# A gated recurrence and an FFT convolution on one core: x2 and its spectrum in halves, the filter with doubled columns, a re-tuned planner

## The chip, the cores and the metric

The kernel runs on one core of a Trainium2 chip. A core has a matrix engine (PE, whose weight loads are listed apart as PEld), a vector engine (DVE), an activation engine (ACT), a general engine (POOL, GpSimd) and a queue that issues transfers (SP). Each engine works off its own instructions in order and waits on semaphores for the others. The metric is the time of one execution on the device, in microseconds.

## The reference

Two layers follow each other. The first is a gated recurrence over time; the second multiplies two projections of its output with a circular convolution of a third, the convolution being written as a product of Fourier transforms over the whole sequence.

```
B, S, D = 4, 6272, 256
sig = 1 / (1 + exp(-f_logit));  f = lb + (1 - lb) * sig;  i = 1 - f
h = 0
for t in range(S):
    h = f[:, t] * h + i[:, t] * x[:, t];  hs[:, t] = h
x1, x2, x3 = split(hs @ w_proj)                      # D -> 3 D
x2 = irfft(rfft(x2, axis=1) * rfft(filter, axis=0))  # length S
out = (x1 * x2 * x3) @ w_out
```

## The kernel before

**The transform.** S = 6272 is split as 128 x 49. A transform over the sequence is a transform of length 128 over m and one of length 49 over r, both written as matrix products with small tables (D1, FT, VA, VB, ID). The 256 channels are kept as pairs: NEP = 128 pairs, cut into 16 units of UE = 8 pairs.

**The stages of a batch.** There are four batches; each goes through these stages:

- `hgrn`: in 13 chunks of 512 steps, f_logit and x are loaded (buffers FL and XT, NX = 4 deep), ACT takes the sigmoid, POOL multiplies it into x, PE turns both to channels by time (L292), ACT makes the forget gate (L304), and a DVE scan (L309) writes h into the two outer parts of HA. POOL then copies each piece into the middle of HA as well (L260, the wraps), so that strided reads can run past the end.
- `phase_p`: 98 matmuls (L587) make x2 for all 49 r and both halves of the channels of h. The weights are h, read with a stride of 49 elements; the moving operand is W2 with 256 columns. DVE or ACT copies the results into X2.
- `phase_f1`: 128 matmuls (L602) transform over m. Their copies fill A, which is the middle of HA: all 16 units lie side by side where the wraps were. `mini` (L617 to L627) then handles the zero frequency of all pairs at once.
- `units`: for each unit, the spectrum of the filter comes from DRAM into Hu, PE transforms over r (L646, F2), DVE multiplies with Hu into PP (L656), POOL fills the zero frequency (L649), PE transforms back over r (L666), and a copy puts the result into Th. Th is a view of X2's memory. Beside the units `gate` works: PE projects h to x1 and x3 (L338), ACT evicts both (L348), and POOL multiplies them into zt (L352). The list GATES says which chunks of the gate go with which unit.
- `phase_o`: in 13 groups of 4 r, PE transforms back over m (L692), DVE multiplies with zt into ys (L699), PE projects with Wo (L709), a copy scales into one of two output buffers, and a store goes out. The first buffer is osb0; the second is the tail of X2, so it appears as X in the profile (`out_dram<-X`).

**Before the first batch** `prepare` builds the tables and the filter's spectrum: it loads the filter, rotates it (L517), transforms it over m with 128 matmuls of 128 columns in fp32r (L531), over r with 64 matmuls (L547), and writes it to DRAM. It shares memory with later stages: raw pieces and results lie in the middle of HA, the transformed filter in a pool that is closed before the buffers of the later stages are opened.

**The order** is not written by hand. Every operation is registered with a guessed cost per engine, the names it reads and writes, and the PSUM banks it takes. `Plan.emit` is a list scheduler: it walks a simulated time, always takes the operation that can start first (ties by the length of the chain that hangs on it, called the level), chooses between ACT and DVE where a copy can run on either, and emits each engine's instructions in that order. `emit` is called twice: once for `prepare` and the first `hgrn`, once for all that follows. The engines then run this fixed order with the real durations. A mis-guessed cost gives an order in which an engine waits with other work queued behind.

Two lines matter for the waits: the copy into X2 also writes the name of the second output buffer, and reads Th.

```
e, both(xv[:, :, r0:r0 + rn]), PS[...]), r=["Th"], w=[("x2", g), ("x2o", g)], src=pp)
r=[("osb", k)] + ([("x2o", i) for i in range(14)] if k else []), kb=128 * rn)
```

Of the kernel before, what the change touches and what calls it, by code (L numbers as in the profile page):

```python
# [9 lines left out]
F32 = mybir.dt.float32  # L10
# [3 lines left out]
AOP = mybir.AluOpType  # L14
# [13 lines left out]
NX = 4  # L28
NCHK = 13

AFTER = (0,)

GATES = [[0, 1, 2], [3, 4], [5, 6], [7, 8], [9, 10], [11, 12]] + [[]] * 10
XR = 10
NEP = 128
# [6 lines left out]
EW = NEP * 128  # L42
# [13 lines left out]
class Plan:  # L56
# [11 lines left out]
    SLACK = 0.0  # L68

    def __init__(self):  # L70
        self.ops, self.writer, self.readers = [], {}, {}
        self.free = {e: 0.0 for e in self.LAT}
        self.bank = [0.0] * 8
        self.dma = 0.0
        self.table = None

    def op(self, cost, fn, r=(), w=(), kb=0.0, table=None, take=0, src=None):
# [9 lines left out]
        if src is not None:  # L87
            preds.add(src)
            self.ops[src]["users"].append(me)
        self.ops.append(dict(cost=cost, fn=fn, preds=preds, kb=kb, table=table, end=None,  # L90
                             eng=None, succ=[], take=take, src=src, users=[], at=None))
# [9 lines left out]
    def ready(self, o, e):  # L101
        at = 0.0
        for p in o["preds"]:
            q = self.ops[p]
            lat = 0.0 if q["kb"] else (self.OWN if q["eng"] == e else self.LAT)[q["eng"]]
            at = max(at, q["end"] + lat)
        return at

    def room(self, n):

        best = None
        for b in range(0, 8, n):
            if None not in self.bank[b:b + n]:
                key = (max(self.bank[b:b + n]), n == 1 and self.bank[b ^ 1] is not None, b)
                if best is None or key < best:
                    best = key
        return best

    def held(self, i):

        return any(self.ops[p]["end"] is None and p != i
                   for j in self.ops[i]["users"] for p in self.ops[j]["preds"])

    def emit(self):
        ops = self.ops
        todo = [i for i, o in enumerate(ops) if o["end"] is None]
        for i in reversed(todo):
            o = ops[i]
            c = min(o["cost"].values()) + (2.6 + o["kb"] / 300.0 if o["kb"] else 0.2)
            o["level"] = c + max((ops[j]["level"] for j in o["succ"]), default=0.0)  # L130
        left = {i: sum(ops[p]["end"] is None for p in ops[i]["preds"]) for i in todo}
        cand = {i for i in todo if not left[i]}
        while cand:
            best = None
            rooms = {n: self.room(n) for n in (1, 2)}
            for e, f in self.free.items():
                can = []
                for i in cand:
                    o = ops[i]
                    if e not in o["cost"]:  # L140
                        continue
                    at = max(f, self.ready(o, e))
                    if o["take"]:
                        if rooms[o["take"]] is None or self.held(i):
                            continue
                        at = max(at, rooms[o["take"]][0])
                    if o["table"] and self.table and o["table"] != self.table:
                        at += 1.3
                    can.append((at, -o["level"], i))
                if can:  # L150
                    first = min(can)[0] + self.SLACK
                    pick = min((c for c in can if c[0] <= first), key=lambda c: c[1:])
                    o = ops[pick[2]]
                    key = (pick[0] + (o["cost"][e] if len(o["cost"]) > 1 else 0.0) * 0.01,
                           pick[1], pick[2], e, pick[0])
                    if best is None or key < best:
                        best = key
            assert best is not None
            i, e, at = best[2:]
            o = ops[i]  # L160
            o["eng"] = e
            o["end"] = self.free[e] = at + o["cost"][e]
            if o["table"]:
                self.table = o["table"]
            if o["kb"]:
                self.dma = max(self.dma, o["end"] + 0.6) + o["kb"] / 300.0
                o["end"] = self.dma + 1.0
            if o["take"]:
                o["at"] = b = rooms[o["take"]][2]
                self.bank[b:b + o["take"]] = [None] * o["take"]  # L170
                o["fn"](e, b)
            elif o["src"] is not None:
                q = ops[o["src"]]
                o["fn"](e, q["at"])
                q["uses"] = q.get("uses", 0) + 1
                q["done"] = max(q.get("done", 0.0), o["end"] + self.LAT[e])
                if q["uses"] == len(q["users"]):
                    self.bank[q["at"]:q["at"] + q["take"]] = [q["done"]] * q["take"]
            else:
                o["fn"](e)  # L180
            cand.remove(i)
            for j in o["succ"]:
                left[j] -= 1
                if not left[j]:
                    cand.add(j)
# [3 lines left out]
def kernel(  # L189
# [35 lines left out]
    A = HA[:, S:S + EW].rearrange("m (e r k) -> m e r k", r=2, k=64)  # L225
# [4 lines left out]
    x1s = konst.tile([128, 2, CH], F32, name="x1s")  # L230
    x3s = konst.tile([128, 2, CH], F32, name="x3s")
# [37 lines left out]
    def hgrn(b):  # L269
        for c in range(NCHK):  # L270
# [6 lines left out]
            for dst, src, t in ((ft, f_logit, ("ft", k)), (xt, x, ("xt", k))):  # L277
                op({"SP": 0.5}, lambda e, dst=dst, src=src, t0=t0, n=n: nc.sync.dma_start(
                    dst, src[b, t0:t0 + n, :].rearrange("(j p) d -> p j d", p=128)),
                   w=[t], kb=n)  # L280
            op({"ACT": 0.1 + 0.213 * nb}, lambda e, ft=ft: nc.scalar.activation(  # L281
                ft, ft, AF.Sigmoid, scale=-1.0), r=["sin"], w=[("ft", k)], table="sigmoid")
            op({"POOL": 0.1 + 0.535 * nb}, lambda e, xt=xt, ft=ft: nc.gpsimd.tensor_tensor(  # L283
                xt, xt, ft, op=AOP.mult), r=[("ft", k)], w=[("xt", k)])

            late = [("U", AFTER[min(c, len(AFTER) - 1)])] if b else []
            for kh in range(2):
                cols = slice(kh * 128, kh * 128 + 128)

                def turn(e, p, src, cols=cols, nb=nb):  # L290
                    for j in range(nb):
                        nc.tensor.transpose(PS[:, p, j * 128:(j + 1) * 128], src[:, j, cols],  # L292
                                            iden[:])
                sT = op({"PE": 0.108 * nb}, lambda e, p, f=turn, s=ft: f(e, p, s),
                        r=[("ft", k), "iden"] + late, w=["qT"], take=1)
                uT = op({"PE": 0.108 * nb}, lambda e, p, f=turn, s=xt: f(e, p, s),
# [6 lines left out]
                op({"ACT": 0.24 + n / 1200.0}, lambda e, p, fT=fT, n=n, kh=kh:  # L303
# [4 lines left out]
                op({"DVE": 0.07 + 2.25 * n / 1000.0}, lambda e, p, h=h, fT=fT, n=n, init=init:  # L308
# [9 lines left out]
                op({"POOL": 0.1 + (z - a) / 1000.0},  # L318
# [5 lines left out]
    def gate(b, u):  # L324
        z = zt
        for c in GATES[u]:
# [4 lines left out]
            for jb in range(2):  # L331
                x13 = []
                for i in range(2):
                    js = slice(i * 256 + jb * 128, i * 256 + jb * 128 + 128)

                    def mm(e, p, js=js, t0=t0, n=n):
                        for kh in range(2):
# [3 lines left out]
                    x13.append(op({"PE": 2 * n / 2400.0}, mm,  # L341
                                  r=hn + ["W13", ("F", u) if u else "qT"], w=["qX"], take=1))
                j = count["s"] % 2
                count["s"] += 1
                xs = [t[:, j, 0:n] for t in (x1s, x3s)]
                for i in range(2):
                    op({"ACT": 0.15 + n / 1200.0}, lambda e, p, xs=xs[i], n=n, i=i:
                       nc.scalar.activation(  # L348
                           xs, PS[:, p, 0:n], AF.Copy, scale=1.0 if i else ZS),
                       w=[("x1s", j, i)], src=x13[i])  # L350
# [438 lines left out]
```

## Time and profile before

| what | value |
|---|---|
| time, median of 3 runs | 593.94 us (581.37 to 595.5) |
| span of the profiled run | 590.6 us |
| PE busy | 505.9 us (86%) |
| DVE busy | 458.7 us (78%) |
| ACT busy | 413.2 us (70%) |
| POOL busy | 391.7 us (66%) |
| moved by DMA | 117.57 MB, mean 199 GB/s |

PE is the busiest engine by this table, but its matmuls are pipelined, so busy time counts the same stretch for several of them and a stretch at a lower clock counts in full. The other engines' busy time can be taken as it stands. The heaviest groups are:

```profile
L352 POOL TENSOR_TENSOR zt<-x1s,x3s 128x490 f16<-128x490 f32 (+1 forms) x104 | 203.8, 1980 | 48.1 <-ACT x3s L348 47.5
L656 DVE TENSOR_TENSOR PP<-PS,Hu 98x1008 f16<-98x1008 f32 x128 | 146.0, 1198 | 8.5 <-ACT x3s L348 3.7
L309 DVE TENSOR_TENSOR_SCAN HA<-fTs,HA,PS 128x512 f16<-128x512 f32 (+1 forms) x96 | 112.3, 1201 | 18.1 <-ACT fTs L304 10.1
L338 PE MATMUL PS<-HA,W 128*128 128x490 f16 (+1 forms) x416 | 101.4, 369 | 5.1 <-ACT X L250 2.7
L531 PE MATMUL PS<-D1r,f 128*128 128x128 f32 x128 | 28.1, 390 | 1.3 <-ACT f L250 1.2
```

A row reads: line, engine, operation, what it writes and reads with shapes, how often, then busy microseconds and the mean nanoseconds of one, then the idle time just before these instructions and what ended most of it. A matmul's mean includes the time it spends in the pipeline, so what one costs in a dense stretch has to be read from the starts of neighbours in the timeline.

### The profile page before, as it was taken

How to read it: one execution, taken by the hardware profiler on the slowest of the kernel's cores; microseconds unless marked ns; L12 is line 12 of the kernel's file. 1: busy time of each engine (PE TensorE's matmuls, PEld its weight loads, DVE VectorE, ACT ScalarE, POOL GpSimd, SP SyncE). 2: the span in 40 equal slices, each digit the busy share in tenths (PEclk: the TensorE clock that was granted, in tenths of full speed). 3: DMA queues.
4: the chain of work that ended last, by engine and by line, in shares of the span. 5: the costliest groups of instructions: out<-in, count | busy, mean ns of one | idle time of the engine just before them, and what ended most of it. 6: DMA issues, size and time to landing. Idle time of an engine off the chain costs nothing.

```text
span 590.6 us, 12576 instructions
## 1 busy us (share of the span) xinstructions
PE 505.9 (86%) x4821; PEld 375.7 (64%) x4821; DVE 458.7 (78%) x442; ACT 413.2 (70%) x577; POOL 391.7 (66%) x362
## 2 busy tenths in 40 slices
PE   1656999988799888698999898888999989989893
PEld 1555777676456788475557775674568878645582
DVE  8776644868798978379999894388988988999761
ACT  4578543569588567687886778786886778878553
POOL 3618640358999847955996778907995783599600
PEclk9978555999999989989999999798999999999897
DMA  8998434492457989900558999103559971045155
GB/s 297 373 360 284 135 111 134 135 307 83 126 156 203 319 264 347 336 1 28 165 168 250 326 369 374 72 1 109 162 172 326 367 279 51 3 136 166 29 214 223
DMA packets 73038, 117.57 MB, mean 199 GB/s; under 512 B 4366, under 2 KB 55634, under 8 KB 72978
## 3 DMA queue, kind: packets, MB, share of 16 engines
q1 hardware_dynamic: 72978, 116.77, 60.0%
q8 instruction: 38, 0.62, 0.5%
q14 instruction: 22, 0.18, 0.1%
HBM read 84.54 MB, written 32.11 MB: 198 GB/s over the span
## 4 chain that ended last, share of the span: by engine, by line
PE 36%; DMA 12%; ACT 8%; DVE 7%; POOL 6%; issue 3%; SPq 0%; ACTq 0%; DVEq 0%
PE PS L338 8%; DMA out_dram<-X 7%; PE PS L666 6%; PE PS L292 6%; POOL zt L352 5%; PE PS L646 5%; PE PS L587 4%; PE PS L709 4%; DMA FL<-in_f_logit_dram 3%; DVE HA L309 2%; ACT X L250 2%; DVE HA L255 2%; PE PS L692 2%; ACT X L252 2%; PE PS L602 1%
## 5 line engine op out<-in xcount | busy, mean ns | idle before, releaser
L352 POOL TENSOR_TENSOR zt<-x1s,x3s 128x490 f16<-128x490 f32 (+1 forms) x104 | 203.8, 1980 | 48.1 <-ACT x3s L348 47.5
L283 POOL TENSOR_TENSOR XT<-XT,FL 128x1024 f32<-128x1024 f32 (+1 forms) x52 | 117.1, 2257 | 55.3 <-ACT FL L281 32.1
L656 DVE TENSOR_TENSOR PP<-PS,Hu 98x1008 f16<-98x1008 f32 x128 | 146.0, 1198 | 8.5 <-ACT x3s L348 3.7
L309 DVE TENSOR_TENSOR_SCAN HA<-fTs,HA,PS 128x512 f16<-128x512 f32 (+1 forms) x96 | 112.3, 1201 | 18.1 <-ACT fTs L304 10.1
L338 PE MATMUL PS<-HA,W 128*128 128x490 f16 (+1 forms) x416 | 101.4, 369 | 5.1 <-ACT X L250 2.7
L250 ACT CAST X<-PS 128x784 f16<-128x784 f32 (+2 forms) x89 | 88.1, 1002 | 12.4 <-PE PS L587 5.5
L304 ACT ACTIVATE fTs<-PS,nomc 128x512 f32<-128x512 f32 (+1 forms) x104 | 68.0, 663 | 40.0 <-PE PS L292 20.6
L348 ACT ACTIVATE x1s<-PS 128x490 f32<-128x490 f32 (+1 forms) x104 | 60.4, 581 | 41.8 <-POOL zt L352 28.3
L260 POOL COPY HA<-HA 128x512 f16<-128x512 f16 (+3 forms) x100 | 58.3, 600 | 32.0 <-DVE HA L309 31.3
L292 PE MATMUL PS<-iden,XT 128*128 128x128 f32 x392 | 65.6, 290 | 11.8 <-POOL XT L283 5.0
L338 PEld LDWEIGHTS <-W 128*128 128x128 f16 x416 | 35.3, 98 | 62.0 <-issue 37.1
L292 PE MATMUL PS<-iden,FL 128*128 128x128 f32 x392 | 65.2, 290 | 7.7 <-ACT FL L281 4.0
L699 DVE TENSOR_TENSOR ys<-PS,zt 128x1024 fp32r<-128x1024 f32 (+1 forms) x52 | 58.8, 1151 | 15.6 <-PE PS L692 11.7
L709 PE MATMUL PS<-Wo,ys 128*128 128x256 f32 x392 | 61.0, 301 | 8.7 <-ACT X L252 4.7
L666 PEld LDWEIGHTS <-PP 98*128 98x128 f16 x1024 | 51.2, 98 | 21.2 <-POOL PP L649 7.2
L255 DVE CAST X<-PS 128x1024 f16<-128x1024 f32 (+2 forms) x27 | 38.7, 1450 | 33.5 <-DMA out_dram<-X 24.1
L281 ACT ACTIVATE FL<-FL 128x1024 f32<-128x1024 f32 (+1 forms) x52 | 52.5, 1011 | 16.5 <-DMA FL<-in_f_logit_dram 16.3
L348 ACT ACTIVATE x3s<-PS 128x490 f32<-128x490 f32 (+1 forms) x104 | 59.9, 576 | 2.9 <-PE PS L338 2.8
L709 PEld LDWEIGHTS PS<-Wo,ys 128*128 128x128 f32 x392 | 51.6, 196 | 15.0 <-ACT X L252 6.0
L292 PEld LDWEIGHTS PS<-iden,XT 128*128 128x128 f32 x392 | 46.6, 147 | 19.6 <-POOL XT L283 6.2
L666 PE MATMUL PS<-VA,PP 98*128 98x98 f16 x512 | 52.8, 208 | 6.3 <-POOL PP L649 3.4
L587 PE MATMUL PS<-W,HA 128*128 128x256 f16 x392 | 50.1, 289 | 9.0 <-ACT X L250 3.9
(91 smaller groups left out, 678.5 us busy)
## 6 DMA issues: line engine op xcount, KB each, us to landing
Hu<-H SPq DMA_DIRECT2D x64, 392.0 KB
FL<-in_f_logit_dram SPq DMA_DIRECT2D x48, 512.0 KB
XT<-in_x_dram SPq DMA_DIRECT2D x48, 512.0 KB
out_dram<-osb SPq DMA_DIRECT2D x24, 512.0 KB
out_dram<-X SPq DMA_DIRECT2D x24, 512.0 KB
HA<-in_moe_filter_fft_dram SPq DMA_DIRECT2D x12, 512.0 KB
H<-HA SPq DMA_DIRECT2D x16, 196.0 KB
H<-HA SPq DMA_DIRECT2D x32, 98.0 KB
```

Of the source, the lines that this page charges most:

```text
L250: nc.scalar.copy(dst, src)
L283: op({"POOL": 0.1 + 0.535 * nb}, lambda e, xt=xt, ft=ft: nc.gpsimd.tensor_tensor(xt, xt, ft, op=AOP.mult), r=[("ft", k)], w=[("xt", k)])
L292: nc.tensor.transpose(PS[:, p, j * 128:(j + 1) * 128], src[:, j, cols], iden[:])
L304: nc.scalar.activation(fT, PS[:, p, 0:n], AF.Identity, scale=nomc[:, kh:kh + 1], bias=1.0),
L309: nc.vector.tensor_tensor_scan(h, fT, PS[:, p, 0:n], init, op0=AOP.mult, op1=AOP.add),
L338: nc.tensor.matmul(PS[:, p, 0:n], W13[:, kh, js], HA[:, HB[kh] + t0:HB[kh] + t0 + n], start=(kh == 0), stop=(kh == 1))
L348: nc.scalar.activation(xs, PS[:, p, 0:n], AF.Copy, scale=1.0 if i else ZS),
L352: zz=z[:, jb, :, m0:m0 + nm]: nc.gpsimd.tensor_tensor(zz, xs[0].rearrange("p (m r) -> p r m", r=Q), xs[1].rearrange("p (m r) -> p r m", r= ...
L587: nc.tensor.matmul(pp[:, r - r0, :], HA[:, n0:n0 + Q * 127 + 1:Q], W2[:, kh, :], start=(kh == 0), stop=(kh == 1))
L656: nc.vector.tensor_tensor(PP[:TB, k, o, :, :, 1:64], px.unsqueeze(1).broadcast_to([TB, 2, UE, 63]), hh[:, :, :, 1:64], op=AOP.mult)
L666: nc.tensor.matmul(PS[:, ib + o, pr * TB:(pr + 1) * TB], PP[:TB, k, o, n, 2 * pr:2 * pr + 2, :], v[:TB], start=(n == 0), stop=(n == 1))
L709: nc.tensor.matmul(po[:, i, :], y[:, kh, i * 128:(i + 1) * 128], Wo[:, kh, :], start=(kh == 0), stop=(kh == 1))
```

## The change

It has six parts.

1. **Own memory.** X2, PP, Hu and zm move out of the late pool into the constant one. Th, the second output buffer and X2 no longer share memory. To pay for it X2 holds only half of the pairs, NX goes from 4 to 3, and A holds four units (NA = 4) in a part of HA's middle that no wrap copy writes.
2. **x2 and its spectrum in halves.** `phase_p(b, v)` makes one half of the channels at a time, with 128 columns of W2, in 7 groups of 7 r. `phase_f1`, `mini` and `unit` follow for the two quarters of that half; each quarter is four units.
3. **The filter's transform over m has doubled columns.** The table D1r is held twice side by side, a matmul has 256 columns, and the copy reads one half of them. Four such matmuls fill two PSUM banks where eight did. The results leave through two buffers in Hu where there were four in HA, and raw pieces have five places where there were six.
4. **One emit.** Filter, first recurrence and all that follows are planned together. The late pool (zt, Th, ys, x1s, x3s, the output buffers) opens inside an operation that waits for the filter's matmuls.
5. **The gate** is free to run wherever the planner puts it: GATES and the waits on units go.
6. **Priorities.** Each operation has a kind, and a table LEAD adds a number per kind and batch to its level. Some guessed costs are new: the gate's product on POOL 0.12 + 3.7 n/1000 in place of 0.12 + 2.2 n/1000 (n = 490), the projection 0.32 per pair in place of 0.34.

The diff, cut to its core:

```diff
-NX = 4
+NX = 3
-GATES = [[0, 1, 2], [3, 4], [5, 6], [7, 8], [9, 10], [11, 12]] + [[]] * 10
+NA = 4
+NP = 2
+NH = 4
+AT = 6144
...
+    LEAD = {
+        "load": (2, 0, -5, -60), "sig": (-10, 21, -13, 0), "u": (9, 12, 0, 85),
...
+            level[i] = way[i] + self.LEAD.get(o["kind"], (0,) * 4)[o["batch"]]
...
-    A = HA[:, S:S + EW].rearrange("m (e r k) -> m e r k", r=2, k=64)
+    A = HA[:, S + AT:S + AT + NA * UE * 128].rearrange("m (e r k) -> m e r k", r=2, k=64)
+    X2 = konst.tile([128, NEP // 2 * PW + 16], F16, name="X2")
+    PP = konst.tile([128, NP, 2, 2, UE, 64], F16, name="PP")
+    Hu = konst.tile([128, NH, 2, 2, UE * 64], F16, name="Hu")
...
-                op({"POOL": 0.12 + 2.2 * n / 1000}, lambda e, xs=xs,
+                op("z", {"POOL": 0.12 + 3.7 * n / 1000}, lambda e, xs=xs, jb=jb, m0=m0, nm=nm:
...
-        hws = [HA[:, S + a:S + a + 1024].rearrange("p (a n) -> p a n", a=2)
-               for a in (6144, 7168, 8192, 9216)]
+        hws = [Hu[:, h, 0] for h in (NH - 2, NH - 1)]
...
-        D1r = tmp.tile([128, 128], F32R, name="D1r")
+        D1r = tmp.tile([128, 2, 128], F32R, name="D1r")
...
-                for i in range(UE):
-                    nc.tensor.matmul(pa[:, i, :], f2[:, (u * UE + i) * PW:(u * UE + i) * PW + 128], D1r[:],
-                                     start=True, stop=True)
+            for h in range(2):
+                def first(e, pb, j=u * UE + h * 4):
+                    pa = PS[:, pb:pb + 2].rearrange("m a (i c) -> m (a i) c", c=256)
+                    for i in range(4):
+                        nc.tensor.matmul(pa[:, i, :], f2[:, (j + i) * PW:(j + i) * PW + 128],
+                                         D1r[:].rearrange("m x k -> m (x k)"), start=True, stop=True)
...
-    def phase_p(b):
-        for g, r0 in enumerate(range(0, Q, 4)):
-                        nc.tensor.matmul(pp[:, r - r0, :], HA[:, n0:n0 + Q * 127 + 1:Q],
-                                         W2[:, kh, :], start=(kh == 0), stop=(kh == 1))
+    def phase_p(b, v):
+        for g in range(7):
+                        nc.tensor.matmul(pp[:, r - 7 * g, :], HA[:, n0:n0 + Q * 127 + 1:Q],
+                                         W2[:, kh, v * 128:v * 128 + 128],
+                                         start=(kh == 0), stop=(kh == 1))
+            pp = op("P", {"PE": 0.118 * 7}, mm, r=hn + E(0, AT) + E(AT + 4096, EW), take=2)
...
+    def spectrum(b):
+        for v in range(2):
+            phase_p(b, v)
+            for q in range(2 * v, 2 * v + 2):
+                for u in range(q * NA, q * NA + NA):
+                    phase_f1(b, u)
+                mini(b, q)
+                for u in range(q * NA, q * NA + NA):
+                    unit(b, u)
...
-        osb = [cv.tile([128, 4, 256], F32, name="osb0"),
-               X2[:, NEP * TB:NEP * TB + 2048].bitcast(F32).rearrange("p (r e) -> p r e", e=256)]
+            late["osb"] = [cv.tile([128, 4, 256], F32, name=f"osb{i}") for i in range(2)]
```

## The prediction

> **What bounds the kernel now.** I read the slices of the whole span first, then the engines' busy time per stage, then the chain of waits and the timeline where the stages look thin, and last single rows for durations.
>
> ```profile
> PE   1656999988799888698999898888999989989893
> DVE  8776644868798978379999894388988988999761
> PEclk9978555999999989989999999798999999999897
> ...
> PE 36%; DMA 12%; ACT 8%; DVE 7%; POOL 6%; issue 3%; SPq 0%; ACTq 0%; DVEq 0%
> ```
>
> One slice is 14.8 us. Slices 5 to 7 (59 to 103 us) have PE at 9 but its clock at 5: that is the filter. DVE drops to 3 and 4 around 240 and 362 us. No engine has more than 36% of the chain: the kernel is not held by one unit but by stages with different limits. By stage (columns: stretch, its length, busy us of PE, PEld, DVE, ACT, POOL, clock, DMA share, GB/s):
>
> ```profile
> 59.00:112.00 53.00, 52.54 (x244) 39.37 (x244) 28.38 (x25) 23.87 (x29) 19.78 (x33) 0.58 0.41 125
> 117.00:252.00 135.00, 115.33 (x1183) 86.43 (x1184) 106.54 (x94) 98.82 (x142) 110.38 (x90) 0.99 0.74 236
> 252.00:379.00 127.00, 115.14 (x1151) 83.36 (x1151) 100.54 (x89) 96.91 (x140) 99.89 (x85) 0.96 0.61 204
> 379.00:490.00 111.00, 102.52 (x1100) 76.59 (x1098) 99.41 (x87) 85.75 (x122) 77.31 (x73) 0.98 0.58 195
> 490.00:590.00 100.00, 85.48 (x941) 61.08 (x939) 74.51 (x65) 65.96 (x93) 52.67 (x45) 0.93 0.33 114
> ```
>
> The head (until the first x2 matmul, L587, at 116 us), then four batches of 135, 127, 111 and 100 us from x2 to x2. The middle ones lose time where x2 is made:
>
> ```profile
> 250.84 2.78 DVE L255 CAST X<-PS 128x1024 f16<-128x1024 f32 x2 [9.59 <-DMA out_dram<-X]
> ...
> 372.58 6.71 PE L587 MATMUL PS<-W,HA 128*128 128x256 f16 x32 [2.71 <-ACT x1s L348]
> 377.96 2.86 DVE L255 CAST X<-PS 128x1024 f16<-128x1024 f32 x2 [14.55 <-DMA out_dram<-X]
> ```
>
> The copies of the new x2 wait until a store of the old output has read its source, because the second output buffer lies in X2; DVE sits idle 9.6 and 14.6 us for it. Ahead of the second one PE also waits for the gate's evictions (x1s), which wait for GpSimd's products at 1.98 us each (L352).
>
> [...] 0.50 from 75 to 105 us although PE is never idle there. [...] the trace has 56 (24 L602 matmuls, from 133.69 to the next start at 135.03) and 113 (95 of L587 in 10.73). [...] the weight loads of L587, read at a stride of 49 elements, take 142 ns, those of L602, contiguous, 98.
>
> ```profile
> L587 PEld LDWEIGHTS <-HA x392: 141/142/168, 116.4 to 501.0; 128*128 128x128 f16 x196
> L602 PEld LDWEIGHTS <-X x512: 95/98/100, 133.7 to 512.8; 128*128 128x128 f16 x171
> ```
>
> **The filter.** Its m-DFT (L531) runs 128 fp32r matmuls of 128 columns:
>
> ```profile
> 69.88 3.68 PE L531 MATMUL PS<-D1r,f 128*128 128x128 f32 x16
> 107.79 1.11 PE L531 MATMUL PS<-D1r,f 128*128 128x128 f32 x8
> ```
>
> At half clock 16 start within 3.47 us (the next row begins at 73.35), 217 ns each; at full clock 8 within 0.95 (next at 108.74), 119 ns. Projection matmuls (L709, same type, 256 columns) take 131 ns (8 from 361.30 to 362.35) in stages whose clock stays at 1.00. So twice the columns cost 12 ns each, and the array streams 256 columns in the slot where it now streams 128. I take it that this keeps the clock up; no row of before shows it directly, so this is the first unknown. Full-clock stage: 128 x 0.131 = 16.8; 64 second-stage matmuls (L547, 4 in 0.63) 10.1; transposes. The instruction order of the changed kernel has 108 transposes between first filter DFT and last against 52, with 92 ahead of it against 128; 108 x 0.11 = 11.9. Sum 38.8 us of PE. DVE and ACT there: 32 copies of 512 columns at 0.65 (the 512-column row of L250 and L255), 16 of 1024 at 1.12, and for 108/8 pieces a scan 1.27, a forget gate 0.69 and half a sigmoid 1.06: 20.8 + 17.9 + 17.1 + 9.3 + 7.2 = 72, or 36 each. With 3 us of slack, 42 us. It starts earlier: 12 input loads stand ahead of the last filter load in the queue against 16, 2.1 MB less at 360 GB/s, so 53.5 us instead of 59.4. First x2 at 95 us instead of 116. At half clock the same PE work is 70 us or more: x2 at about 120. Only two buffers (in Hu) remain for the filter's results against four; a pair must go out within 2 x 2.6 us. A store held back in the SP queue by a load that waits for one of only 3 input buffers would hold the second-stage matmuls behind it. I allow that in the range.
>
> **A batch, by engine.** DVE: scans 122.1/4 = 30.5, products 36.5, y 14.7, zero frequency 2.5 before and about 5 after (12 short instructions in place of 3, at 0.3 to 0.6). ACT: forget gate 17.0, x1 and x3 30.1, sigmoid 13.1. Shared copies: x2 18.7, A 17.1, Th 13.1, output 12.8; x2 becomes 14 of 896 columns in place of 13, the same. Sum 206 before, 208 after, so 104 each. POOL: (203.8 + 117.1 + 58.3 + 23.4)/4 = 101; the wipe of X2's gaps per batch (0.4) goes. PE at its start-to-start times: transposes 196 x 0.11 = 21.6, x1 and x3 104 x 0.207 = 21.5, x2 98 x 0.113 = 11.1, F1 128 x 0.056 = 7.2, F2 64 x 0.126 = 8.1, inverse 256 x 0.044 = 11.3 and 196 x 0.035 = 6.9, projection 98 x 0.131 = 12.8: 100.5. Here the change adds: x2 becomes 196 matmuls of 128 columns with 196 strided weight loads. The matmul alone would give 0.056; but its load takes 142 ns, and the transposes, whose loads take 140, run at 0.11. So 11 to 21.8 us; I take 0.085, 16.7, and PE 106 a batch. That is the bound of a batch.
>
> **What the edits release.** Own output and Th buffers remove the 9.6 and 14.6 us waits above. X2 in halves and four slots of A that no wrap copy overlaps let units start when a quarter of the spectrum is there, and let scans and their copies of the next batch run beside units. The order shows this: when the first output inverse (L692) is issued, 88 to 112 of the next batch's 196 transposes are done, against 24 to 52 before. What now stands at 50 to 66 us of transposes, scans and loads (DMA share 0.9) shrinks to some 35 us. GpSimd's product is planned at 1.93 us instead of 1.20, near the measured 1.98, so that fewer evictions stand in ACT's and PE's queue ahead of x2. zt and Th stay single: gate products of a batch wait for the last y before. The priorities cost no instruction; their worth is the bubble that remains. Before, a batch with PE work 100.5 took 111 at best (379 to 490), 10% over; with the handover shorter I take 6% over 106: 112 us, three times. The last batch has no transposes behind it and was 100 us; with 5.6 of x2 and a little less at its start, 103; its output (19 us of PE beside stores, clock 0.8) stays exposed.
>
> **The sum.** 95 + 3 x 112 + 103 = 534 us.
>
> **Rivals.** (1) The filter's clock stays at half: 120 + 336 + 103 = 559. For it: half clock with a PE that is never idle; against: projection stages at 1.00. (2) GpSimd's chain takes the place of the old waits: gate products only after the last y, 26 x 1.98 = 51.5, plus slots 5.9 and half of u and wraps 22 make 79 us, then an output stage of 35 and a handover of 6: 120 a batch, 95 + 360 + 103 = 558; strided loads at 0.142 (PE 117 a batch) give the same. For it: POOL already 15.0 of 15 us busy from 285 to 300. (3) Better: slack 2%, x2 at 0.06, head 90: 90 + 3 x 105 + 100 = 505. (4) No gain: half clock and the GpSimd chain with stalls of the shallower buffers, 120 + 3 x 124 + 105 = 597, slower than before. For it: every engine is then loaded to 100 of some 105 us, so that any wrong guess of the fixed order becomes a stall; against: the units stages now run 34.7 of 35 us PE-busy (405 to 440).
>
> **Numbers.** Forecast (518 to 548) 0.50, rivals 1 and 2 (548 to 582) 0.27, rival 3 0.10, rival 4 0.13, half of it within 2% and half beyond (2% is 582 and 606 us). Range 510 to 575: from near rival 3 to rivals 1 and 2 with a stall more. Faster 0.87, same 0.07, slower 0.06.
>
> **What would show it.** Clock near 1.0 through the filter and the first x2 at 95; x2's matmuls at 56 to 110 ns; no wait of x2's copies for a store; x2 to x2 of 112; POOL near 95% while gate products run. Wrong, if the filter stays at 0.5, or if the x2-to-x2 times stay above 120.

## The result and the profile after

The changed kernel took 563.49 us (median; 560.7 to 564.64) beside 587.65 us (578.35 to 595.5) for the kernel before on the same chip. The ratio is 0.971, interval [0.963, 0.979]: faster by 2.9%. The kernel before takes 571 to 582 us in most executions and up to 599 us in the others; its profile (590.6 us) is of the second kind while the ratio compares the first, so that the gain is some 17 us by the ratio and 28 us between the profiles. The forecast was 534 us.

The slices and the chain of waits of the changed kernel:

```profile
span 562.9 us, 13418 instructions
...
PE   1567798899989898999969998999989999999774
...
DVE  7998468497898877598999897979999897889753
...
PEclk9989999899999989999998999999999999999999
DMA  8995778751658889632667989324879852324055
...
PE 33%; DMA 7%; DVE 6%; issue 4%; ACT 3%; POOL 3%; POOLq 0%; ACTq 0%; DVEq 0%; SPq 0%
```

The clock row has no stretch of 5 any more. The DMA row has slices of 7 to 9 ahead of every later x2 (12 to 15, 21 to 24 and 28 to 31, counted from 0; one is 14.1 us) and slices of 2 and 3 after it. The kernel before had the same pattern, with slices down to 0 in between:

```profile
DMA  8998434492457989900558999103559971045155
```

By stage, cut within 0.7 us of the first x2 matmul of each batch (same columns as before: length, PE, PEld, DVE, ACT, POOL, clock, DMA share, GB/s):

```profile
103.50:229.00 125.50, 114.38 (x1270) 87.06 (x1269) 102.66 (x99) 95.09 (x139) 98.80 (x82) 0.97 0.67 212
229.00:345.60 116.60, 107.69 (x1220) 81.20 (x1218) 101.57 (x94) 92.06 (x132) 92.17 (x79) 0.99 0.66 211
345.60:461.20 115.60, 108.79 (x1257) 83.89 (x1256) 106.52 (x100) 90.24 (x133) 93.14 (x79) 1.00 0.66 210
461.20:562.90 101.70, 86.58 (x1072) 62.87 (x1072) 73.54 (x73) 68.85 (x97) 52.31 (x42) 0.99 0.37 130
```

The waits of the engines (who waited, for whom; total us, times, longest us):

```profile
POOL zt L397 <- ACT x3s L393: 32.6, 21, 4.3
...
ACT FL L327 <- DMA FL<-in_f_logit_dram: 22.7, 22, 2.9
POOL XT L329 <- DMA XT<-in_x_dram: 22.4, 14, 3.3
ACT osb L298 <- DMA out_dram<-osb: 19.6, 16, 3.6
DVE X L301 <- PE PS L637: 18.7, 23, 2.8
```

The copies of x2 (L301) now wait for PE alone. Their waits of 9.6 and 14.6 us for a store are gone, as meant. What still waits for stores is ACT's copy into the output buffers, 19.6 us in 16 waits, none over 3.6 us. The loads of f_logit and x stand third and fourth in the list: each wait is short, none over 3.3 us, which is why no single gap points at them.

The next table has the start of the first x2 and the time from one batch's first x2 to the next, as the traces show them, with the forecast and the runs told below (us; the last column runs to the end):

| kernel | first x2 | batch 0 | batch 1 | batch 2 | last |
|---|---|---|---|---|---|
| forecast | 95 | 112 | 112 | 112 | 103 |
| before | 116.4 | 126.1 | 130.1 | 117.3 | 100.8 |
| before, doubled columns | 95.5 | 129.7 | 126.9 | 118.6 | 99.4 |
| changed | 103.9 | 124.4 | 117.2 | 115.5 | 101.8 |
| no priorities | 105.4 | 143.8 | 128.6 | 127.1 | 106.1 |
| three engines relieved | 105.8 | 121.6 | 111.5 | 108.9 | 94.2 |
| half loads | 105.6 | 113.9 | 108.7 | 111.4 | 100.7 |
| no loads | 102.8 | 112.6 | 108.0 | 111.3 | 102.7 |

### The profile page after: what moved, and what is told of

Its sections match the earlier page's. It is cut to its first block, busy times and chain, and to the rows that moved or that the text cites. A ratio compares the mean times of both kernels' runs of the same rounds, so it can differ in the third digit from the quotient of the medians.

```text
span 562.9 us, 13418 instructions
## 1 busy us (share of the span) xinstructions
PE 487.2 (87%) x5261; PEld 369.4 (66%) x5261; DVE 464.1 (82%) x483; ACT 414.9 (74%) x592; POOL 392.2 (70%) x356
## 4 chain that ended last, share of the span: by engine, by line
PE 33%; DMA 7%; DVE 6%; issue 4%; ACT 3%; POOL 3%; POOLq 0%; ACTq 0%; DVEq 0%; SPq 0%
PE PS L381 8%; PE PS L637 6%; DMA out_dram<-osb 5%; PE PS L336 4%; PE PS L772 4%; PE PS L720 4%; PE PS L700 3%; PE PS L651 3%; DVE PP L710 2%; DMA FL<-in_f_logit_dram 2%; ACT osb L298 2%; POOL zt L397 2%; DVE ys L760 1%; PE PS L754 1%; DVE HA L353 1%
## 5 line engine op out<-in xcount | busy, mean ns | idle before, releaser
L397 POOL TENSOR_TENSOR zt<-x1s,x3s 128x490 f16<-128x490 f32 (+1 forms) x104 | 200.8, 1945 | 45.2 <-ACT x3s L393 32.6
L381 PE MATMUL PS<-HA,W 128*128 128x490 f16 (+1 forms) x416 | 108.0, 374 | 4.6 <-ACT x1s L393 1.2
L306 POOL COPY HA<-HA 128x512 f16<-128x512 f16 (+3 forms) x100 | 59.8, 618 | 26.8 <-DVE HA L353 25.2
L298 ACT ACTIVATE osb<-PS 128x1024 f32<-128x1024 f32 (+1 forms) x47 | 46.3, 985 | 35.0 <-DMA out_dram<-osb 19.6
L336 PE MATMUL PS<-iden,XT 128*128 128x128 f32 x392 | 64.3, 286 | 6.9 <-POOL XT L329 3.6
L296 ACT CAST HA<-PS 128x1024 f16<-128x1024 f32 x54 | 54.6, 1014 | 10.4 <-PE PS L651 9.0
L381 PEld LDWEIGHTS <-W 128*128 128x128 f16 x416 | 36.6, 99 | 35.6 <-issue 16.3
L336 PEld LDWEIGHTS PS<-iden,FL 128*128 128x128 f32 x392 | 47.5, 146 | 16.4 <-issue 5.7
L637 PEld LDWEIGHTS <-HA 128*128 128x128 f16 x784 | 52.9, 152 | 2.8 <-issue 0.5
```

Of the source, the lines that this page charges most:

```text
L381: nc.tensor.matmul(PS[:, p, 0:n], W13[:, kh, js], HA[:, HB[kh] + t0:HB[kh] + t0 + n], start=(kh == 0), stop=(kh == 1))
L397: nc.gpsimd.tensor_tensor(late["zt"][:, jb, :, m0:m0 + nm], xs(0).rearrange("p (m r) -> p r m", r=Q), xs(1).rearrange("p (m r) -> p r m", ...
L637: nc.tensor.matmul(pp[:, r - 7 * g, :], HA[:, n0:n0 + Q * 127 + 1:Q], W2[:, kh, v * 128:v * 128 + 128], start=(kh == 0), stop=(kh == 1))
```

## The experiments

**The reference point.** The kernel before, unedited.

> The kernel before, once more, with a profile: is the clock of 0.5 through the filter (59 to 112 us) a trait of its 128-column matmuls or of that one execution? Theory 1 (mine: columns set the clock): again near 0.5 from 60 to 105 us, first x2 at 116 us. Theory 2 (the execution's own): clock near 1.0 there, the filter some 15 to 20 us shorter, first x2 near 100 us, total near 578 us; then a fair part of my forecast gain was never there to be had.

581.22 us (575.1 to 597.96), ratio 1.001 [0.998, 1.005]. The profile, of an execution of 594.43 us, again shows the filter at half clock:

```profile
PEclk9968555898989999979999999899999999999997
```

**The doubled columns**, in the kernel before (D1r twice as wide, four matmuls for two banks, copies of 512; the order is planned anew):

```diff
-        D1r = tmp.tile([128, 128], F32R, name="D1r")
+        D1r = tmp.tile([128, 2, 128], F32R, name="D1r")
...
-                    nc.tensor.matmul(pa[:, i, :], f2[:, (u * UE + i) * PW:(u * UE + i) * PW + 128], D1r[:],
+                        nc.tensor.matmul(pa[:, i, :], f2[:, (j + i) * PW:(j + i) * PW + 128],
+                                         D1r[:].rearrange("m x k -> m (x k)"), start=True, stop=True)
```

> The kernel before with one part of the change: the filter's transform over m with doubled columns (four matmuls to two banks, copies of 512 columns). Theory 1 (in this kernel, with a filter stage of few other matmuls, the columns decide whether the clock stays up): clock near 1.0 from 59 to 105 us, none of the executions near 592 us that the kernel before has, time 570 to 578 us. Theory 2 (columns do nothing, as in the changed kernel): clock near 0.5 again in the profile, time as before.

570.35 us (568.81 to 571.77), ratio 0.989 [0.985, 0.992]. The clock row, and the weight loads of x2, whose first starts at 95.3 us:

```profile
PEclk9978999988999999999999999998999999999997
...
L593 PEld LDWEIGHTS <-HA x392: 141/142/167, 95.3 to 482.1; 128*128 128x128 f16 x196
```

With twice the columns, in groups of four, the array keeps its clock: 9 in the slices from 57 to 114 us, where the row above has 5. The profile loses 20.9 us ahead of the first x2, but the ratio is worth only 6 to 7 us. The mean clock of whole executions fits with that: 0.966 to 0.972 in these four, 0.958 to 0.962 in the ones of the kernel before that the ratio compares, and 0.927 in its first profile, where the filter's stretch alone (0.58 over 53 us) takes 0.038 off the mean. By this estimate most of the 21 us could not be had in the executions compared. None of those was profiled, so where their clock falls isn't shown.

**The columns back to 128 in the changed kernel.**

```diff
-                        nc.tensor.matmul(pa[:, i, :], f2[:, (j + i) * PW:(j + i) * PW + 128],
-                                         D1r[:].rearrange("m x k -> m (x k)"), start=True, stop=True)
+                        nc.tensor.matmul(pa[:, i, 0:128], f2[:, (j + i) * PW:(j + i) * PW + 128],
+                                         D1r[:, 0, :], start=True, stop=True)
```

> The changed kernel, same order, but the filter's transform over m with 128 columns (only the half that is read is computed). Theory 1 (columns keep the clock up): clock near 0.5 from 50 to 103 us, x2 10 us later or more, total 10 us more or more. Theory 2 (no influence): clock as with 256 columns, total within 2 us, since PE has slack in this stage.

562.19 us, ratio 0.974 [0.967, 0.981], with a clock of 0.96 from 49 to 96 us all the same. Here the columns make no difference. The filter's matmuls now come in groups of four between transposes and waits, as the timeline of the changed kernel shows, and in this order the clock stays up without the columns:

```profile
62.08 0.74 PE L580 MATMUL PS<-D1r,f 128*128 128x256 f32 x4 [1.15 <-ACT Hu L298]
...
67.36 0.74 PE L580 MATMUL PS<-D1r,f 128*128 128x256 f32 x4 [1.81 <-ACT Hu L298]
```

The groups of four and the smaller copies came into the kernel before together with the columns. So the columns aren't shown as the cause there either: no run had 256 columns in groups of eight, or 128 columns in groups of four in the old order.

**No priorities** (`LEAD = {}`).

> The changed kernel with an empty table LEAD: same operations and buffers, other order. If the structure (own buffers, halves) carries the gain: 563 to 572 us. If the tuned priorities carry it: at or above the time before, 580 us or more.

614.57 us, ratio 1.064 [1.055, 1.072]: slower than the kernel before. The memory layout and the halves without the table lose; the order that the table makes is worth 50 us, and 42 of the 48 us between the profiles lie in the three batches.

**Four buffers for the filter's results**, laid in HA, first with the order planned anew, then with the names that the planner goes by left alone, so that the order stays (the edit of the first):

```diff
-        hws = [Hu[:, h, 0] for h in (NH - 2, NH - 1)]
+        hws = [HA[:, S + a:S + a + 1024].rearrange("p (a n) -> p a n", a=2)
+               for a in (6144, 7168, 8192, 9216)]
...
-            hw, ht = hws[u % 2], [("Hu", NH - 2 + u % 2)]
+            hw, ht = hws[u % 4], E(6144 + 1024 * (u % 4), 6144 + 1024 * (u % 4) + 1024)
```

> The changed kernel with the filter's results leaving through four buffers in the middle of HA, as before, instead of two in Hu. In the changed kernel ACT and DVE wait 18.5 us for these writes, with PE queued behind. If the two buffers hold the filter stage (50 to 103 us): the wait falls below 4 us, first x2 at 92 to 96 us, total 8 to 11 us less. Rival (the stage is held by input loads and the chain transpose, gate, scan): x2 at 101 or later, total within 3 us.

> The changed kernel with four buffers for the filter's results, and the order of every engine kept exactly as in the changed kernel. If the two buffers hold the filter stage: ACT's and DVE's wait for H<-Hu (18.5 us) gone, first x2 5 to 9 us earlier than 103.5, total 5 to 9 us less. If the stage is held by the input loads: x2 and total within 2 us. It also tells whether the loss in the run with four buffers and a new order came from the order.

582.06 us, ratio 1.003 [1.000, 1.007], with the new order; 563.57 us, 0.975 [0.968, 0.982], with the old one. The two have the same instructions and buffers, so the 18 us between them (17 by the ratios) are order alone. With the old order the waits for the results' buffers are gone, and the first x2 comes at 103.0 instead of 103.9: PE then waits at the filter's last matmuls, behind a product of GpSimd that waits for a load.

```profile
100.08 0.59 PE L614 MATMUL PS<-mX,FTr 64*98 64x128 f32 x4 [2.13 <-POOL mX L589]
```

**A fourth input buffer during the first recurrence** (in two slots of Hu that are idle then), on top of that:

```diff
-            xt, ft = XT[:, k, 0:nb], FL[:, k, 0:nb]
+            xk = count["x"] % 4 if count["x"] < 11 else (count["x"] - 11) % 3
+            xt, ft = [(Hu[:, h].rearrange("p a b n -> p (a b n)").bitcast(F32).rearrange("p (j d) -> p j d", d=D)
+                       if xk == 3 else t[:, xk])[:, 0:nb] for t, h in ((XT, 2), (FL, 3))]
```

> The changed kernel, same order, with four buffers for the filter's results (as in the run before) and a fourth input buffer during the first recurrence, laid in memory that is idle then. If the head is now held by the inputs (in the run with four result buffers PE's last filter matmul waits for GpSimd, whose queue stands at a multiply that waits for its load): first x2 at 95 to 98 us instead of 103, total 5 to 8 us less. If the chain of the order itself holds it: x2 at 102 or later, total within 2 us.

561.01 us, ratio 0.972 [0.964, 0.981]. Nothing is gained; its profile, of an execution at a mean clock of 0.96, has the first x2 at 103.8.

**The zero frequency's sums on GpSimd** (`nc.gpsimd.tensor_tensor` in place of `nc.vector.tensor_tensor` for zm, L683).

> The changed kernel, same order, with the 16 sums of the zero frequency (zm<-zp, 1506 ns each on DVE, 24 us in all) on GpSimd. If DVE's time bounds the batches: 8 to 20 us less. If DVE has slack or GpSimd is the tighter engine: within 3 us. The 1506 ns would be explained by a wait for GpSimd inside the instruction if the same sum takes 0.3 to 0.5 us there.

561.79 us, ratio 0.976 [0.971, 0.981]. DVE's busy time falls from 464.1 to 441.5 us, and the time is the same within the interval.

**Ten of thirteen stores of each batch left out** (`g % 6 == 0 and nc.sync.dma_start(...)`).

> The changed kernel, same order, with 10 of 13 stores of the output left out in each batch (those groups of the output are not written). 39 of 103 MB of input and output traffic in the output stages go. If transfers bound the output stages (DMA share 0.9 there): each batch 5 to 8 us shorter, total 20 us or more less beyond the 5 us of the last stores. If the engines bound them: 5 to 8 us less in all, at the tail.

556.48 us, ratio 0.966 [0.957, 0.975]: 7 us less by the medians, 3 by the ratios, and 8 us in the three batches of the profile (348.8 instead of 357.1). By the profiles 21 MB of stores are gone, not the 39 MB that the expectation names. In the 45 us ahead of the third x2 the DMA share falls from 0.94 to 0.82, and PE starts 506 matmuls there instead of 486. The total is far from the 20 us expected if all transfers bound alike; but what is gained lies in the batches and not at the tail, where the last one is 1 us shorter.

**One engine relieved in batches 1 to 3**, order kept: half the columns of x1 and x3 for PE (`n // q`, q = 2), half the rows of the gate product for GpSimd (`nm // 2`), half the columns of the spectrum products for DVE (`1:32` for `1:64`).

> The changed kernel, same order, in which x1 and x3 of batches 1 to 3 are projected for half of the columns only: 104 matmuls a batch at about 0.105 us instead of 0.207, so 10.6 us of PE work less in each (of 103). If PE bounds the batches: those from x2 to x2 fall from 117 and 115 to 107, total 25 us or more less. If PE has slack: total within 6 us.

> The changed kernel, same order, in which GpSimd multiplies half of the gate's rows in batches 1 to 3 (25 us of its 100 a batch less). If GpSimd's chain (gate products only after the last y, then before the next output stage) bounds the batches, as my second rival had it: 6 us or more off each, total 20 us less. If not: within 6 us in total.

> The changed kernel, same order, in which DVE forms half of the spectrum's products in batches 1 to 3 (32 products a batch at 0.65 us instead of 1.19: 17 us of some 106 less). If DVE bounds the batches: 6 us or more off each, total 20 us less. The run with the zero-frequency sums on GpSimd speaks against it: then within 6 us in total. If all three of these runs stay within 6 us, no single engine holds the batches, and what is left is the waits between them in the fixed order.

560.71 us (0.973 [0.963, 0.983]), 556.97 us (0.971 [0.962, 0.980]) and 560.63 us (0.971 [0.961, 0.982]): 3, 6 and 3 us by the medians. By the ratios, which take out that the kernel before ran 4 to 5 us shorter on this chip, it is nothing. Neither PE nor GpSimd nor DVE by itself bounds the batches. ACT, busy for 90 to 95 us of a batch, was not relieved.

**All three at once, the loads left out, and everything together:**

```diff
-                op("load", {"SP": 0.5}, lambda e, dst=dst, src=src, t0=t0, n=n: nc.sync.dma_start(
+                op("load", {"SP": 0.5}, lambda e, dst=dst, src=src, t0=t0, n=n: b == 0 and nc.sync.dma_start(
```

> The changed kernel, same order, with three reliefs at once in batches 1 to 3: half the columns of the x1 and x3 matmuls, half of the gate products' rows, half of the spectrum products' columns (part of the computation is left out). Alone they gave 3, 6 and 3 us. If different engines bound different stretches in turn, removing all three gives clearly more than the sum: 530 to 542 us. If each saving is swallowed by what nothing here touches (loads, transposes, scans, handovers), the gains only add: 550 us or a little above.

> The changed kernel, same order, with the loads of x and f_logit left out in batches 1 to 3 (the buffers keep old values; the output is not the reference's). About 38 MB of loads go, and the waits of ACT (22.7 us) and GpSimd (22.4 us) for them in three batches. If the three input buffers or the DMA queue hold the batches: 10 us or more off each of three batches, 530 us. If the batches are held by handovers between queues of in-order work, of which the loads are one of many: 553 to 560 us, like each of the other reliefs.

> The changed kernel, same order, with the three reliefs, the loads of batches 1 to 3 and ten of thirteen stores of each batch left out. If engines and transfers take turns: 500 to 520 us, since PE's remaining 90 us per batch would then be the bound. If the handovers in the written order are the hold by themselves: not below 535.

The three reliefs: 547.64 us (0.952 [0.939, 0.964]), 16 us less than the changed kernel by the medians, where the single ones add to 12; by the ratios it is 11 where they add to nothing. It lies between the two expectations, and whether the reliefs only add stays open. No loads: 538.66 us (0.934 [0.926, 0.942]), 25 us less (22 by the ratios). All with few stores: 512.68 us (0.888 [0.879, 0.897]), 51 us less (48), where the parts add to 48 (36). So the loads are the largest single hold, about as large as the three engines and the stores together.

**Half of every load**, with their number, the waits for a buffer and the place in the queue kept:

```diff
-                op("load", {"SP": 0.5}, lambda e, dst=dst, src=src, t0=t0, n=n: nc.sync.dma_start(
-                    dst, src[b, t0:t0 + n, :].rearrange("(j p) d -> p j d", p=128)),
+                op("load", {"SP": 0.5}, lambda e, dst=dst, src=src, t0=t0, n=n // 2 if b else n: nc.sync.dma_start(
+                    dst[:, 0:n // 128] if n >= 128 else dst[:, 0, 0:128], src[b, t0:t0 + n, :].rearrange("(j p) d -> p j d", p=128) if n >= 128 else src[b, t0:t0 + 128, 0:128]),
```

> The changed kernel, same order, with every load of x and f_logit of batches 1 to 3 cut to half of its rows (the other half of the buffer keeps old values; the output is not the reference's). The number of loads, the waits for one of three buffers and the place in the queue stay; only the bytes are halved, 6.4 MB less per batch. Without these loads the kernel took 539 us. If the transfers' own time holds the batches: 540 to 548 us. If it is the waits for a free buffer and the in-order queue, which the bytes don't touch: 555 us or more.

542.01 us (541.4 to 542.52), ratio 0.940 [0.929, 0.951]: 21 of the 25 us (18 of 22 by the ratios). So it is the bytes of the loads, or the packets that carry them, that hold the batches, and not the number of loads. The same 45 us ahead of the third batch's x2, in the changed kernel, with half the loads, and with none:

```profile
300.30:345.60 45.30, 42.31 (x486) 34.16 (x483) 40.12 (x36) 35.24 (x51) 37.41 (x35) 1.00 0.94 309
```

```profile
282.80:328.10 45.30, 44.01 (x513) 36.26 (x511) 43.50 (x39) 37.38 (x55) 41.28 (x38) 1.00 0.71 232
```

```profile
278.00:323.30 45.30, 44.82 (x518) 36.92 (x516) 44.18 (x40) 37.99 (x56) 41.94 (x40) 1.00 0.36 134
```

The second last column falls from 0.94 to 0.71 and 0.36, and in the same 45.3 us PE starts 513 and 518 matmuls instead of 486, and DVE is busy 43.5 and 44.2 us instead of 40.1. In the changed kernel the transfers hold this stretch back: it moves 309 GB/s at a DMA share (the mean over the 16 DMA engines) of 0.94. With PE, GpSimd or DVE relieved, or all three, the same stretch still moves 299 to 309 GB/s at 0.91 to 0.94; less work for the engines doesn't raise that. Neither the share nor the rate is a fixed ceiling: in steps of 5 us from 300 to 345 the share runs from 0.77 to 1.05 and the rate from 236 to 377 GB/s.

Half the bytes do one thing more: a load that lands sooner also lets its buffer go sooner. From the first x2 stage to the last the queue waits 87 us in all for PE's transposes to free an input buffer in the changed kernel, 71 us with half loads, and 55 us in the kernel before with its four buffers. So the rate of the transfers and the depth of three buffers aren't separated by this run.

**The stores in ACT's queue** (`nc.scalar.dma_start`), so that loads don't stand behind stores that wait.

> The changed kernel complete, same order, but the output stores are issued from ACT's queue, where the evictions that they wait for mostly run, and no longer stand in SP's queue ahead of the loads. SP waits 92 us for those evictions in the changed kernel. If loads are held by standing behind stores that wait: 5 us or more faster, 552 to 558 us. If the loads are held by their buffers or by the transfers: within 3 us of 563; if ACT's own work is delayed by 52 issues: slower, 565 to 570 us.

569.55 us (560.82 to 572.34), ratio 0.980 [0.956, 1.003]; its profile spans 559.0. The scatter is wider than the effect asked for. A gain of 5 us or more in the median isn't there; more can't be said.

**Another table of priorities**, found for costs nearer to the measured ones (zero frequency 2.1 us instead of 0.75, x2's matmuls 0.93 for 0.83, its copies 1.1). Only the order differs:

```diff
+        fixed = {"zm": {"DVE": 2.1}, "P": {"PE": 0.93}, "x2": {"ACT": 1.1, "DVE": 1.1},
+                 "slot": {"POOL": 0.33}}
+        add = {"scan": 0.05, "FF": 0.1, "y": 0.02}
...
-        "load": (2, 0, -5, -60), "sig": (-10, 21, -13, 0), "u": (9, 12, 0, 85),
+        "load": (2, -187, -192, 326),
+        "sig": (-286, -86, -198, -475),
+        "u": (299, 85, -9, -147),
...
```

> The changed kernel complete, with another table of priorities, found for costs nearer to the measured ones (zero frequency 2.1 us in place of 0.75, x2's matmuls 0.93 in place of 0.83 per piece, its copies 1.1, sigmoid and scans a few per cent longer). Only the order of the same instructions differs. If better costs in the planner carry over to the chip: 548 to 556 us. If the loads' transfers and the waits that the planner doesn't see set the batches, an order tuned on costs of the engines gives nothing or loses: 560 to 570 us.

563.56 us, ratio 0.974 [0.966, 0.983]: the same time with a quite different order. No version run here is clearly faster than the changed kernel with all of its work done.

## Why the prediction was right and wrong

**The sum.** The direction was right, the size was not. Forecast 95 + 336 + 103 = 534; profile 103.9 + 357.1 + 101.8 = 562.8. Of the 29 us, 21 lie in the three batches and 9 in the head; the last batch was 1 us better.

**The step that failed: the slack of a batch.** The forecast let the stretch of transposes, scans and loads shrink from 50 to 66 us to "some 35 us", and wrote its DMA share of 0.9 beside it without drawing the consequence. It counted PE, DVE, ACT and POOL for a batch and no bytes. By the profile's issues a batch loads 12 pieces of 512 KB and one of 128 for x and again for f_logit (12.8 MB), stores as much as one of them (6.4) and reads 16 filter spectra of 392 KB (6.4). Nothing in the change makes these fewer, and of the 13 pairs of loads and 13 stores that a batch has, 9 pairs and 9 stores are issued in the 45 us ahead of the third x2 (300.3 to 345.6). The stretch did not shrink to 35 us: four slices of 7 to 9 in the DMA row, some 56 us, still stand ahead of each later x2. The time that the loads cost stood at nothing in the sum. With half of their bytes the three batches took 113.9 + 108.7 + 111.4 = 334.0 us, with none 331.9, instead of 357.1: the missing term is 23 us in the profiles, 21 by the medians, 18 by the ratios.

Bytes don't all count alike: in the three batches 16 MB fewer of stores brought 8 us, 19 MB fewer of loads 23. Whether the loads hold by their rate or by the time for which they keep one of three buffers stays open. More buffers, which might spread the bytes into the thin slices, weren't tried in the batches.

**The yardstick of that slack.** That 334 meets the 336 of the forecast is in part luck, since two more terms were off. The forecast's batches of 135, 127, 111 and 100 us were cut at 117, 252 and 379, but the first x2 of the middle ones stand at 242.5 and 372.6; from x2 to x2 the kernel before took 126.1, 130.1, 117.3 and 100.8. The "111 at best, 10% over" PE's 100.5 was thus 117.3, or 17% over, and the changed kernel's second and third batch (117.2 and 115.5) are hardly shorter than that. And PE's work was set 4 us too high (x2's matmuls, below): 334 us are 9% over three times 102, not 6% over 106.

**The head: 103.9, not 95.** The clock did stay up (0.97 from 49.7 to 103.9). The filter's transforms over m started at 49.7, 4 us sooner than the 53.5 of the forecast (which counted the loads at 360 GB/s; the kernel before moves 358 from 10 to 50 us), and the last of them started at 95.9, 46 us later, about where the forecast had the whole stage end (53.5 + 42). Then 8 us pass until x2, for which the forecast had nothing: in them PE does the last transposes, second-stage matmuls with a wait of 1.6 us for a result buffer, and six matmuls of the gate (2.4 us) that the order puts ahead of x2. I had named the two result buffers as a risk "in the range"; the changed kernel shows waits of 2.1 and 2.6 us for them at the end, but four buffers (first x2 at 103.0), a fourth input buffer as well (103.8), and no loads of later batches (102.8) each leave the time where it was. The kernel before with the columns has its first x2 at 95.5 in its own order. What holds the head of the new order isn't settled.

**The clock.** Right in its result, open in its reason: the kernel before with the columns has the clock up and x2 at 95.5 instead of 116.4 to 118.7, but in the changed kernel groups of four with 128 columns have it up too. That the columns keep the clock up was my assumption. What sets the clock was not shown: in the kernel before PE was busy for all of the 30 us from 75 to 105 at 0.50, so a busy PE was not enough here. And the forecast took the profile's half clock as a trait of the kernel before and so counted 21 us of head, of which the ratio shows 6 to 7 with the columns in the kernel before.

**x2's matmuls.** Forecast 0.085 us each, taken between 0.056 and 0.11. In a dense stretch they run at 66 ns although each loads strided weights that take 152 on average:

```profile
345.64 6.46 PE PS L637 x98
```

98 in 6.46 us; a batch pays 12.9 us instead of 16.7. This miss went the other way by 4 us a batch and brought nothing that shows; 10 us less of PE work a batch in another place brought nothing clear either.

**The releases.** The waits of x2's copies for stores went, as forecast. What they were worth can't be had from the batch times of the kernel before with columns (474.5 us for all four) and the changed one (458.9) alone: the 16 us between them are the whole net effect of memory, halves and order, and without the tuned priorities that effect is a loss.

**The rivals.** The first (clock at half) fell. The second (the GpSimd chain, 558 us) came close in number with a wrong cause: a gate product of half the size brought 6 us by the medians and nothing by the ratios. The third fell with the loads. The fourth, in which "any wrong guess of the fixed order becomes a stall", didn't come about with this table, but is what happens without it (615) and with a slightly different plan (582, no faster than before).

## What to carry to other kernels

Put the bytes of a stage into the same table as the engines' busy time, and take a stretch like the one here, 45 us at a DMA share of 0.94, as a likely bound until a run says otherwise: many waits of 1 to 3 us for loads look harmless in the list and cost some 20 us together here. In a kernel whose order is written ahead, compare an edit with the order held fixed and with the order made anew; the order alone moved the same instructions by 18 and by 50 us. When relief of any one engine gives almost nothing, halve the bytes next. And cut the stages of a profile at the instruction that begins them, as a slack read from cuts 6 us off is 6 us wrong.

## What the runs showed of the hardware

The zero frequency's sum stretches on DVE beside products of GpSimd. It takes 0.22 us at best there, but its median is 1.45 and its longest 4.52 in the changed kernel; on GpSimd it is steady (minimum, median, maximum in ns):

```profile
L683 DVE TENSOR_TENSOR zm<-zp x16: 224/1450/4521, 118.7 to 518.1; 98x128 f16<-98x128 f16 x16
```

```profile
L683 POOL TENSOR_TENSOR zm<-zp x16: 418/430/491, 120.2 to 513.0; 98x128 f16<-98x128 f16 x16
```

The longest, from 288.59 to 293.11, lies beside these instructions of GpSimd, start and length first:

```profile
288.48 0.34 POOL L703 COPY PP<-zm 98x32 f16<-98x32 f16 x1
288.63 0.63 POOL L306 COPY HA<-HA 128x512 f16<-128x512 f16 x1
289.20 3.83 POOL L397 TENSOR_TENSOR zt<-x1s,x3s 128x490 f16<-128x490 f32 x2
```

They end at 293.03, and the sum 0.08 us later: it lasted through two copies and two gate products that follow each other without a gap. Of the 16 sums 14 end 0.08 or 0.09 us after a product of GpSimd, and the two that overlap none take 0.22 and 0.23 us. The cause was not shown. The same is seen in the head: the casts of the weights, 0.29 to 0.30 us when GpSimd rests, take 2.3 to 2.5 us beside three of its products, each ending 0.15 to 0.17 us after one of them:

```profile
18.45 2.34 DVE L437 CAST W<-HA 128x256 f16<-128x256 f32 x1
20.71 2.47 DVE L441 CAST W<-HA 128x128 f16<-128x128 f32 x1
23.01 2.47 DVE L437 CAST W<-HA 128x256 f16<-128x256 f32 x1
```

```profile
18.03 7.30 POOL L329 TENSOR_TENSOR XT<-XT,FL 128x1024 f32<-128x1024 f32 x3 [11.90 <-ACT FL L327]
```

So DVE's busy time can't quite be taken as it stands: of the 24 us of these sums some 3.6 would be left if each took its least (16 times 0.22, an estimate). It didn't show in the time here: moving the sum away changed nothing clear (561.79 us beside 563.49), and neither did halving the spectrum's products on DVE (560.63).
